# Stacking high and low halves of the step arguments, with a new channel order and re-ordered instruction lists

## The chip, the cores and the metric

The kernel runs on one core of a Trainium2 chip. The metric is the device time of one launch in microseconds (us); it is some 1.8 us longer than the span from the first to the last instruction in the trace. Every kernel was run several times. Each run has a state: "slow" where it lies over 1.5% above the fastest run of the same kernel, "fast" otherwise, and the trace of each run gives the mean clock that TensorE was granted. Comparisons here use fast runs only, unless said. Engines are named as the profile names them: PE is the matmul engine, PEld its weight loads, DVE the vector engine, ACT the scalar engine, POOL GpSimd, SP the queue that issues most DMAs.

## The reference, cut to what matters

The kernel computes a state-space layer as a long convolution, a one-row expert, and a gate:

```python
xn = _layernorm(A_u)                                  # 2048 rows x 512 channels
dt = exp(log_dt)[:, None];  A = A_re + 1j * A_im      # 512 channels x 128 states
P = exp((dt * A)[:, :, None] * arange(2048))          # step arguments dt*A, times the tap number
K = einsum("dn,dnl,dn->dl", Cc, P, dt * Bc).real      # taps
y = irfft(rfft(xn padded to 4096) * rfft(K padded)) + xn * Dskip
g = silu(xn + scatter_add(expert of the one row with the largest xn @ w_r))
return A_u + y * g
```

(The text above shortens the reference; inputs are bf16.) The taps `K` are not computed one by one. An exponent and a sine of `dt*A*l` are factored into products of small tables, and the two Fourier transforms are matmuls against tables.

## The kernel before: the parts that matter here

The kernel is written as a list of operations, and each engine's instruction order is fixed by a hand-tuned list of numbers. A helper at one line (L187) issues almost every matmul, so the profile shows them by their tiles. Four parts matter.

The step arguments are `dt*A`, which bf16 alone would not hold precisely enough. So a high half and a low half (the rest) are made for each group of channels, and a matmul adds them up in PSUM, once per half:

```python
for gp in range(4):
    ts(AD[:, pi, 0, gp, :], S[:, gp, :], DT4[:, gp:gp + 1], MUL, 128, 4)                        # high
for gp in range(4):
    stt(AD[:, pi, 1, gp, :], S[:, gp, :], DT4[:, gp:gp + 1], AD[:, pi, 0, gp, :], MUL, SUB, 128) # low
# ...
def args(pi, c, pair):
    q, js = c // 2, c % 2
    rs = slice(32 * q, 32 * q + 32)
    for gp in range(4):
        o = sap(PB, 0, 128, 512 * (2 * pair + gp // 2) + 16 * (gp % 2), [[32, 16], [1, 16]])
        for hl in range(2):
            mms.append((o, AD[rs, pi, hl, gp, :], IDIJ[rs, 16 * js:16 * js + 16, :], hl == 0, hl == 1))
```

`PB` is the kernel's one PSUM tile, declared as 128 partitions by eight banks of 512 fp32 words; `sap(tile, partition, partitions, offset, pattern)` writes an access pattern by hand as steps and counts.

The taps come out of `kgen` into `KT`, are turned once more through PSUM, and are copied to `KT2` in SBUF as bf16:

```python
for nj, bank in ((6, 4), (5, 5), (5, 4)):
    # ... matmuls of GG and QQ into PB[:, bank]
    act(KT[:, :, j0:j0 + nj], PB[:, bank, 0:80 * nj].rearrange("p (a b) -> p b a", b=80), ACT.Copy, 80 * nj)
# ...
act(KT2[:, q, :, 64 * js:64 * js + 64], PB[:, 5, 0:320].rearrange("p (t c) -> p t c", t=5), ACT.Copy, 320)
```

The profile leaves buffer numbers out, so `KT2` is printed as `KT`.

The spectrum of the taps is 640 matmuls of `KT2` by the table `W` (rows `PB<-KT,W`), each with 128 output columns; ACT then copies a bank pair to `K2T`, DVE multiplies it by the signal's spectrum (`PAB<-U,K2T`), and further matmuls (`PB<-PAB,FA`) transform back:

```python
kp, ip = 1, 3
def pos(pair, i):
    return PB[:, 2 * pair + nd * i // 512, nd * i % 512:nd * i % 512 + nd]
for u2 in range(nu):
    for ro in range(2):
        for k in range(5):
            mms.append((pos(kp, 2 * u2 + ro), W[:, nu * tg + u2, ro, k, :],
                        sap(KT2, 0, 128, d0 // 128 * 640 + 128 * k, [[640, nd // 128], [1, 128]]), k == 0, k == 4))
act(ko, PAIR[kp].rearrange("p a b -> p (a b)"), ACT.Copy, 1024)
```

Here the output, `pos(...)`, is a run of 128 neighbouring fp32 words.

The last part is the tail: after the last inverse transform, a result `ZT` goes to DRAM (`scr_z`), is read back transposed (`DD`), goes through the last matmuls and the gate, and is written out.

Of the kernel before, what the change touches and what calls it, by code (L numbers as in the profile page):

```python
# [8 lines left out]
ALU = mybir.AluOpType  # L9
# [40 lines left out]
class _Graph:  # L50
# [154 lines left out]
    def dma(self, eng, pairs, **kw):  # L205
        fns, outs, ins = [], [], []
        nd = 0
        cost = 0.0
        for dst, src, *ft in pairs:
            fns.append(lambda e, dst=dst, src=src: e.dma_start(dst, src))  # L210
            outs.append(ft[0] if ft else dst)
            ins.append(ft[1] if ft else src)
            cnt = 1
            for s, c in list(dst.ap):
                cnt *= c
            run = min(_run(dst), _run(src))
            nd += cnt // run
            cost += cnt // run * max(33.0, 8.0 + run * mybir.dt.size(dst.dtype) / 25.0) / 16.0
        each = 500.0 if eng == PO else 450.0
        n = self.add(eng, fns, outs, ins, each * len(pairs) + (0.3 * nd if eng == PO else 0.0), dma=True, nbytes=cost, **kw)  # L220
        n.nd = nd
        return n

    def schedule(self):
# [12 lines left out]
        for _ in nodes:  # L237
# [6 lines left out]
            if n.dma:  # L244
                a = max(dma_free[e], n.end)
                dma_free[e] = a + n.nbytes + sum(min(n.nbytes, max(0.0, dma_free[o] - a)) for o in ENGS if o != e)
                n.end = dma_free[e] + 2000.0
# [146 lines left out]

def _pstart(ap):
    return ap.offset // _row(ap.tensor)

_FILL = [(6, 2, 5), (7, 2, 2), (34, 4, 2), (44, 4, 3), (45, 4, 3), (52, 4, 5), (55, 4, 1), (69, 2, 2), (70, 2, 1),
         (107, 4, 1), (129, 4, 2), (216, 2, 6)]
_ORDER = {  # L400
    "sync": [
        11, 0, 1, 2, 12, 10, 15, 3, 13, 14, 5, 4, 8, 9, 16, 6, 7, 152, 157, 162, 167, 324, 325, 326, 308, 327, 323, 318, 313,
        353, 373, 363, 383, 516, 547, 513, 515, 548, 452, 462, 514, 482, 472, 559, 666, 667, 566, 635, 645, 655, 665, 678, 754,
        786, 785, 764, 774, 784, 805, 807, 806, 808, 685, 804, 797, 821, 830,],
    "scalar": [
        20, 21, 44, 52, 53, 56, 23, 55, 48, 58, 59, 62, 61, 50, 108, 80, 109, 81, 119, 130, 121, 129, 149, 172, 169, 127, 151,
        154, 175, 159, 178, 181, 156, 184, 187, 164, 190, 305, 161, 273, 166, 274, 310, 307, 312, 315, 290, 289, 317, 241, 320,
        329, 279, 322, 333, 331, 232, 337, 230, 237, 243, 341, 281, 283, 412, 413, 286, 287, 295, 297, 299, 335, 302, 339, 303,
        348, 428, 343, 358, 352, 429, 368, 418, 420, 422, 362, 425, 426, 434, 436, 438, 441, 442, 378, 372, 486, 494, 495, 447,
        533, 535, 536, 457, 382, 539, 538, 467, 541, 542, 451, 492, 545, 544, 546, 550, 549, 461, 551, 477, 594, 593, 518, 471,  # L410
        610, 609, 481, 522, 599, 520, 601, 603, 712, 606, 607, 615, 526, 617, 713, 619, 524, 530, 622, 623, 528, 668, 630, 669,
        670, 640, 728, 532, 810, 650, 634, 729, 644, 718, 660, 720, 722, 654, 726, 725, 734, 736, 738, 741, 749, 664, 759, 788,
        753, 769, 763, 779, 742, 773, 783, 787, 789, 809, 811, 818, 814, 823, 827,],
    "vector": [
        65, 22, 25, 24, 27, 28, 26, 31, 30, 29, 66, 69, 63, 70, 67, 93, 64, 68, 91, 95, 97, 94, 92, 98, 96, 33, 99, 71, 34, 72,
        100, 42, 73, 101, 35, 74, 102, 37, 104, 76, 32, 105, 77, 41, 38, 106, 78, 36, 107, 79, 39, 46, 43, 40, 82, 103, 75, 45,
        110, 87, 83, 84, 86, 90, 89, 113, 85, 123, 122, 88, 111, 124, 125, 134, 133, 115, 131, 136, 112, 135, 132, 138, 114,
        140, 142, 137, 118, 139, 247, 141, 116, 144, 146, 143, 147, 145, 249, 248, 117, 250, 252, 251, 253, 254, 255, 256, 192,
        193, 257, 258, 194, 259, 196, 198, 199, 200, 201, 260, 203, 261, 205, 206, 262, 276, 264, 263, 265, 266, 211, 267, 268,
        210, 275, 270, 292, 269, 271, 207, 208, 277, 291, 228, 229, 233, 231, 234, 238, 240, 284, 293, 300, 414, 415, 416, 386,  # L420
        388, 387, 389, 390, 391, 392, 394, 393, 395, 396, 397, 349, 398, 350, 399, 400, 401, 402, 403, 359, 404, 360, 405, 406,
        407, 409, 408, 410, 385, 430, 423, 431, 432, 369, 370, 439, 484, 379, 380, 487, 488, 498, 490, 489, 499, 496, 501, 497,
        500, 507, 502, 503, 504, 505, 449, 506, 567, 511, 448, 508, 509, 512, 510, 569, 568, 570, 572, 571, 458, 573, 574, 575,
        459, 576, 577, 578, 469, 579, 580, 581, 582, 468, 583, 584, 595, 585, 554, 587, 586, 479, 557, 588, 478, 590, 596, 589,
        561, 591, 597, 564, 612, 604, 611, 613, 714, 562, 620, 555, 558, 686, 688, 687, 689, 691, 690, 692, 693, 694, 565, 695,
        715, 696, 697, 625, 698, 716, 631, 699, 673, 700, 701, 632, 676, 703, 702, 704, 706, 705, 680, 641, 642, 707, 709, 708,
        710, 683, 652, 651, 731, 723, 730, 732, 662, 661, 739, 751, 750, 677, 681, 674, 761, 760, 770, 771, 780, 781, 744, 802,
        799, 800, 792, 795, 684, 796, 803, 793, 819, 820, 815, 816, 824, 828, 829, 825,],
    "gpsimd": [
        17, 221, 213, 222, 223, 212, 19, 215, 214, 220, 235, 18, 244, 245, 246, 552, 671, 812, 790,],  # L430
    "tensor": [
        51, 54, 47, 57, 60, 49, 128, 120, 148, 150, 171, 168, 126, 153, 170, 174, 177, 158, 173, 180, 176, 155, 183, 179, 186,
        182, 163, 185, 189, 188, 304, 160, 191, 272, 165, 195, 309, 197, 306, 288, 202, 314, 204, 311, 209, 316, 319, 216, 217,
        218, 219, 224, 225, 226, 227, 278, 328, 321, 411, 332, 330, 336, 334, 282, 340, 236, 239, 242, 280, 285, 294, 296, 298,
        427, 301, 338, 346, 344, 345, 347, 342, 354, 356, 355, 357, 351, 364, 366, 367, 365, 384, 361, 374, 417, 419, 376, 421,
        375, 424, 433, 377, 435, 437, 371, 440, 493, 483, 485, 443, 445, 446, 444, 381, 534, 455, 453, 454, 456, 537, 491, 463,
        465, 466, 464, 540, 450, 473, 543, 475, 553, 460, 474, 476, 592, 556, 517, 470, 608, 560, 480, 521, 563, 598, 519, 600,
        602, 711, 525, 605, 614, 616, 618, 529, 523, 727, 621, 527, 628, 629, 626, 627, 624, 672, 636, 638, 639, 637, 531, 675,
        646, 648, 649, 647, 679, 633, 656, 657, 682, 643, 658, 717, 659, 719, 721, 653, 724, 733, 735, 737, 663, 740, 745, 747,
        748, 746, 757, 755, 758, 756, 752, 767, 765, 766, 768, 762, 775, 776, 777, 778, 772, 782, 743, 801, 791, 794, 798, 817,  # L440
        813, 822, 826,],
# [113 lines left out]
def build(nc, A_u, A_A_re, A_A_im, A_B_re, A_B_im, A_C_re, A_C_im, A_log_dt, A_Dskip,  # L555
# [27 lines left out]
    with g.ctx:  # L583
# [35 lines left out]
        LD4 = place("LD4", [128, 4], BF16)  # L619
        DT4 = place("DT4", [128, 4], F32)  # L620
# [24 lines left out]
        ERU = place("ERU", [128, 4, 1408], BF16, o_w + 29696)  # L645
        WD = place("WD", [128, 11, 512], BF16, o_w + 29696)
        ERG = place("ERG", [128, 4, 1408], BF16, o_w + 40960)
# [4 lines left out]
        SAI = place("SAI", [128, 4, 128], BF16, o_b + 8192)  # L652
        EP1 = place("EP1", [128, 4, 256], F32, o_b + 9216)
        WW1 = place("WW1", [128, 2, 256], F32, o_b + 13312)
        UPD = place("UPD", [16, 512], BF16, o_b + 13312)
        SN1 = place("SN1", [128, 4, 256], F32, o_b)
        CN1 = place("CN1", [128, 4, 256], F32, o_b + 4096)
        CS1 = place("CS1", [128, 2, 256], F32, o_b + 7168)
        ZA1 = place("ZA1", [128, 256], F32, o_b + 8192)
        ZB1 = place("ZB1", [128, 256], F32, o_b + 15360)  # L660
# [3 lines left out]
        T1 = place("T1", [128, 2, 256], F32, o_k)  # L664
        T2 = place("T2", [128, 2, 256], F32, o_k + 2048)
# [3 lines left out]
        AD = place("AD", [128, 2, 2, 4, 128], BF16)  # L669
        o_q = cur[0]  # L670
        QQ = place("QQ", [128, 2, 2, 64, 32], BF16)
        WW0 = place("WW0", [128, 2, 256], F32, o_q + 8192)
        ZB0 = place("ZB0", [128, 256], F32, o_q + 8192 + 2048)
        o_g = cur[0]
        EP0 = place("EP0", [128, 4, 256], F32, o_g)
        SN0 = place("SN0", [128, 4, 256], F32, o_g + 4096)
        CS0 = place("CS0", [128, 2, 256], F32, o_g + 8192)
        CN0 = place("CN0", [128, 4, 256], F32, o_t)
        ZA0 = place("ZA0", [128, 256], F32, o_t + 4096)
        POW = ((EP0, SN0, CN0, WW0, (ZA0, ZB0), CS0), (EP1, SN1, CN1, WW1, (ZA1, ZB1), CS1))  # L680
        GG = place("GG", [128, 1, 2, 20, 128], BF16)
        KP = place("KP", [128, 2, 64], BF16)
# [44 lines left out]
        def ts(o, a, s1, op, n, mode=1, s2=None, op2=None):  # L727
            ins = [a] + ([s1] if not isinstance(s1, (int, float)) else [])
            if len(ins) > 1 and mode == 4:
                n, mode = 40 + 1.55 * n, 4  # L730
# [589 lines left out]
```

## Time and profile before

| | before |
|---|---|
| time, median of 4 runs | 198.47 us (197.09 to 200.85) |
| span in the trace | 198.6 us, granted clock 0.925 (a further run, of 200.38 us) |
| first spectrum group starts | 78.80 us |
| last inverse burst starts | 181.14 us |
| PE busy between these | 91.67 of 102.30 us |

The traced run, at 200.38 us, lies 1.7% above the fastest of the four. It is 2.4 us longer than the mean of the three fast ones (198.01), and so may its stretches be in all. The rows of the groups of instructions that the change touches most are these. The columns are line, engine, operation, output and inputs, shapes, count; then busy us and mean ns of one; then the idle time just before these instructions and what ended it.

```profile
L187 PE MATMUL PB<-KT,W 128*128 128x128 bf16 x640 | 39.7, 219 | 2.7 <-ACT K2T L754 1.7 <-ACT KT L754 0.5 <-ACT KV L754 0.2
L187 PE MATMUL PB<-CA,AD 32*128 32x256 bf16 x128 | 20.9, 317 | 8.2 <-DVE AD L738 6.5 <-ACT EE L754 0.8 <-ACT QQ L754 0.8
L725 DVE TENSOR_TENSOR PAB<-U,K2T 128x1024 bf16<-128x1024 bf16 x32 | 21.2, 685 | 12.8 <-ACT K2T L754 11.8 <-DMA scr_a<-AT 1.0
```

The spectrum and the argument matmuls are the two large consumers of PE. The mean of 219 ns is not the distance between two matmuls, as they overlap: a burst of 40 at 78.80 us lasts 2.41 us, and with some 0.22 us for the last one that is 56 ns from one to the next. DVE waits 12.8 us before these products, 11.8 of it for a spectrum that is not there yet, so DVE isn't what holds this stage.

### The profile page before, as it was taken

The page shows a single profiled execution, that of the slowest core. Times are in us where ns is not written, and L with a number is a line of the kernel's source. Part 1 is how long each engine was busy: PE and PEld are TensorE (multiplying, and loading weights), DVE is VectorE, ACT ScalarE, POOL GpSimd, SP SyncE. Part 2 cuts the span into 40 slices and gives each one's busy share as a digit, 9 for nine tenths or more (in the row PEclk, how much of TensorE's full clock was granted, in tenths as well). Part 3 has the DMA queues.
Part 4 walks back from the last instruction along what each step waited for, and adds up shares of the span by engine and source line. Part 5 has one row for each costly group of instructions (what it writes and reads, how often), then busy time and mean ns, then how long its engine had stood idle before and what let it go on. Part 6 is the DMA issues. An engine that isn't in the chain of part 4 may idle for free.

```text
span 198.6 us, 5566 instructions
## 1 busy us (share of the span) xinstructions
PE 165.8 (83%) x2411; PEld 120.2 (61%) x2411; DVE 143.5 (72%) x339; ACT 144.7 (73%) x186; POOL 13.9 (7%) x24
## 2 busy tenths in 40 slices
PE   0697997799998779888999985998899987896960
PEld 0463665555865247877887853676677866894320
DVE  2889889986940239799389999778999980633473
ACT  2298599996749197775799999889969793656440
POOL 0046000000050200000000000200020030000000
PEclk9999999996969957999999999579999999998597
DMA  5979943336969999410031696542833249467965
GB/s 147 333 228 413 418 187 106 108 95 168 316 201 332 430 394 395 133 42 16 3 76 36 163 333 174 153 125 63 263 78 90 56 103 209 119 168 209 226 158 144
DMA packets 40666, 36.79 MB, mean 185 GB/s; under 512 B 26593, under 2 KB 35938, under 8 KB 39746
## 3 DMA queue, kind: packets, MB, share of 16 engines
q1 hardware_dynamic: 38178, 22.25, 39.0%
q0 software_dynamic: 2464, 14.19, 19.9%
q8 instruction: 19, 0.31, 0.6%
q14 instruction: 5, 0.04, 0.1%
HBM read 25.95 MB, written 10.49 MB: 183 GB/s over the span
## 4 chain that ended last, share of the span: by engine, by line
PE 36%; DVE 21%; ACT 18%; DMA 17%; issue 2%; SPq 2%; DVEq 0%; ACTq 0%
PE PB L187 33%; DMA scr_a<-AT 10%; ACT AT L754 4%; ACT XT L957 4%; DVE TT L725 4%; DVE PAB L725 4%; ACT KT L754 4%; DMA X<-in_A_u_dram 3%; DVE ST L802 3%; DVE GG L725 2%; SPq L210 2%; DMA DD<-scr_z 2%; PE PB L280 2%; ACT K2T L754 2%; ACT QQ L754 2%
## 5 line engine op out<-in xcount | busy, mean ns | idle before, releaser
L187 PE MATMUL PB<-KT,W 128*128 128x128 bf16 x640 | 39.7, 219 | 2.7 <-ACT K2T L754 1.7
L187 PEld LDWEIGHTS PB<-KT,W 128*128 128x128 bf16 x640 | 35.9, 98 | 6.1 <-ACT K2T L754 3.4
L187 PE MATMUL PB<-CA,AD 32*128 32x256 bf16 (+1 forms) x192 | 25.9, 357 | 9.9 <-DVE AD L738 8.2
L725 DVE TENSOR_TENSOR PAB<-U,K2T 128x1024 bf16<-128x1024 bf16 x32 | 21.2, 685 | 12.8 <-ACT K2T L754 11.8
L725 DVE TENSOR_TENSOR TT<-GG,ZB 128x512 bf16<-128x512 bf16 (+2 forms) x64 | 27.8, 470 | 0.6
L187 PEld LDWEIGHTS PB<-CA,AD 32*128 32x128 bf16 x192 | 17.4, 129 | 16.7 <-DVE AD L738 9.1
L754 ACT ACTIVATE K2T<-PB 128x1024 bf16<-128x1024 f32 x16 | 16.4, 1022 | 10.6 <-PE PB L187 10.6
L754 ACT ACTIVATE KT<-PB 128x400 bf16<-128x400 f32 (+2 forms) x32 | 18.4, 576 | 5.9 <-PE PB L187 5.2
L187 PE MATMUL PB<-PAB,FA 64*128 64x128 bf16 x512 | 18.7, 228 | 2.1 <-DVE PAB L725 2.1
L725 DVE TENSOR_TENSOR QQ<-QQ,EE 128x2048 bf16<-128x2048 bf16 x16 | 19.5, 1219 | 0.2
L754 ACT ACTIVATE ZT<-PB 128x1024 bf16<-128x1024 f32 x16 | 16.3, 1018 | 4.2 <-PE PB L187 4.1
L187 PEld LDWEIGHTS PB<-PAB,FA 64*128 64x128 bf16 x512 | 15.8, 100 | 5.3 <-DVE PAB L725 2.4
L754 ACT ACTIVATE AT<-PB 128x1024 bf16<-128x1024 f32 x16 | 16.5, 1074 | 1.9 <-PE PB L187 1.8
L754 ACT ACTIVATE U<-PB 128x1024 bf16<-128x1024 f32 x16 | 16.1, 1027 | 1.8 <-PE PB L187 1.6
L725 DVE TENSOR_TENSOR GG<-TT 128x512 bf16<-128x512 bf16 (+2 forms) x32 | 15.1, 472 | 0.6
L754 ACT ACTIVATE EE<-PB 128x1024 bf16<-128x1024 f32 x16 | 15.4, 1035 | 0.0
L187 PE MATMUL PB<-GG,QQ 128*128 128x80 bf16 x256 | 14.2, 213 | 1.4 <-ACT XSEL L754 0.7
L187 PE MATMUL PB<-DD,CB 128*128 128x512 bf16 x32 | 10.9, 458 | 4.4 <-DVE TF L725 2.3
L187 PEld LDWEIGHTS PB<-GG,QQ 128*128 128x128 bf16 x256 | 11.9, 106 | 4.0 <-ACT XSEL L754 1.0
L187 PE MATMUL PB<-XN,CB 128*128 128x256 bf16 (+1 forms) x80 | 12.8, 297 | 1.3 <-ACT AT L754 1.3
L802 DVE BATCH_NORM_STATS2 ST<-X 128x6 f32<-128x512 bf16 x16 | 9.9, 683 | 5.1 <-DMA X<-in_A_u_dram 5.1
L280 PE MATMUL PB<-CA 128*128 128x512 bf16 x33 | 13.3, 524 | 0.1
(131 smaller groups left out, 225.1 us busy)
## 6 DMA issues: line engine op xcount, KB each, us to landing
W<-c_w POOLq DMA_DIRECT2D x4, 1280.0 KB, 10.0
scr_a<-AT SPq DMA_DIRECT2D x8, 512.0 KB, 6.0
BT<-scr_a SPq DMA_DIRECT2D x8, 512.0 KB, 5.3
scr_z<-ZT SPq DMA_DIRECT2D x16, 256.0 KB, 3.5
DD<-scr_z SPq DMA_DIRECT2D x6, 512.0 KB, 5.1
XR<-in_A_u_dram POOLq DMA_DIRECT2D x4, 512.0 KB, 6.0
out_dram<-XR SPq DMA_DIRECT2D x8, 256.0 KB, 2.9
X<-in_A_u_dram SPq DMA_DIRECT2D x3, 512.0 KB, 6.6
```

Of the source, the lines that this page charges most:

```text
L187: fns.append(lambda e, o=o, l=l, r=r, st=st, sp=sp, tp=tp: e.matmul(o, lhsT=l, rhs=r, start=st, stop=sp, tile_position=tp, skip_group_chec ...
L210: fns.append(lambda e, dst=dst, src=src: e.dma_start(dst, src))
L280: n.fns = [lambda e, o=o: e.matmul(o, lhsT=lhs, rhs=rhs, start=True, stop=True, tile_position=(0, 0), skip_group_check=True)] * k
L725: g.V(lambda e: e.tensor_tensor(out=o, in0=a, in1=b, op=op), [o], [a, b], n, mode)
L754: nd = g.A(lambda e: e.activation(out=o, in_=i, func=func, **kw), [o], ins, n + (110 if "bias" in kw else 0), after=[ph["pre"]] if tab els ...
L802: g.V(lambda e, b=b: e.bn_stats(ST[:, b, :], X0[:, b, :]), [ST[:, b, :]], [X0[:, b, :]], 512)
L957: g.A(lambda e, pv=pv, xt=xt: e.activation(out=xt, in_=pv, func=ACT.Copy), [XT[:, bq % 2]], [PB[:, bank, :]], 1024)
```

## The change

The intent is to shorten PE's work on the arguments. The high and low halves of `dt*A` are placed on different partitions of one tile, so that one matmul over 64 rows adds both, and two groups of channels run in two row tiles at a time. The taps are copied in two pieces instead of three per chunk, an extra product on DVE goes, layernorm and power operations are merged, and the power stages, the sines and the expert move ahead of the first spectrum. The stacked load brings the channels in as even ones, then odd ones, and this order is undone where the spectrum is written. The core of the diff, with cuts marked:

```diff
+        def sload(S, A):
+            for gh, eng in ((0, SP), (1, AC)):
+                g.dma(eng, [(S[64 * gh + 32 * hl:64 * gh + 32 * hl + 32].rearrange("p (q e) n -> p q (e n)", q=4),
+                             dap(A, 8192 * gh, [[256, 32], [16384, 4], [1, 256]])) for hl in range(2)])
 ...
+            for c in range(8):
+                act(HH[:, pi, c, :], S[:, c, :], ACT.Copy, 128, scale=DTS[:, c:c + 1])
+                stt(AD[:, pi, c, :], S[:, c, :], DTM[:, c:c + 1], HH[:, pi, c, :], MUL, SUB, 128)
 ...
         def args(pi, c, pair):
-            (four groups, high and low half: eight matmuls of 256 columns)
+            g.M([(PB[:, 2 * pair + gh, :], AD[64 * gh:64 * gh + 64, pi, c, :], IDIJ[64 * gh:64 * gh + 64, :, :], True, True) for gh in range(2)])
 ...
         def kgen(c):
-            for nj, bank in ((6, 4), (5, 5), (5, 4)):
+            for hg in range(2):
 ...
-            tt(kp, gl, sap(QQ, 0, 128, 4096 * qb + 31, [[2048, 2], [32, 64]]), MUL, 128, 1)
 ...
         def spec(pt):
-                kp, ip = 1, 3
+                kp, ip = (2 if pt == 3 and tg % 2 else 1), 3
 ...
-                            mms.append((pos(kp, 2 * u2 + ro), W[:, nu * tg + u2, ro, k, :],
+                            mms.append((sap(PB, 0, 128, 1024 * kp + nd * (2 * u2 + ro), [[1, 2], [2, 64]]), W[:, nu * tg + u2, ro, k, :],
 ...
 (program: bcw(1), powers(1), the sines and the expert before the first f2 and spec; all five lists of instruction order replaced)
```

(The line in parentheses under `args` stands for six removed lines, and so does the last one for the order of calls and the lists.)

## The prediction

> **What bounds the kernel now.** I read the engines' shares first, then busy time by stretch, then the chain of waits, then single bursts in the timeline. The page's first part:
>
> ```profile
> PE 165.8 (83%) x2411; PEld 120.2 (61%) x2411; DVE 143.5 (72%) x339; ACT 144.7 (73%) x186; POOL 13.9 (7%) x24
> ```
>
> No engine is full over the whole span, so I cut it where the character changes: the first spectrum burst (PB<-KT,W, the taps times the table W) starts at 78.80 us, the last inverse burst (PB<-PAB,FA) at 181.14. Columns: stretch, length, then busy us and instruction count for each engine, granted clock, DMA share, GB/s.
>
> ```profile
> core 0: us, PE busy (x) PEld busy (x) DVE busy (x) ACT busy (x) POOL busy (x), PEclk, DMA share, GB/s
> 3.60:78.80 75.20, 63.74 (x685) 41.81 (x686) 54.68 (x161) 55.58 (x72) 9.06 (x16) 0.91 0.77 274
> 78.80:181.10 102.30, 91.67 (x1662) 74.30 (x1660) 81.16 (x161) 82.13 (x104) 4.63 (x4) 0.97 0.46 125
> 181.10:198.60 17.50, 10.34 (x66) 4.11 (x66) 7.67 (x18) 5.70 (x9) 0.00 (x0) 0.74 0.70 173
> ```
>
> The reader should see that in the middle stretch, over half of the kernel, PE is busy 91.67 of 102.30 us, at nearly full clock: it is the fullest engine there, and DVE and ACT have 21 and 20 us to spare. The first stretch is a mix (loads, layernorm, the router and the expert, waits for DMA); the last is a serial tail. The chain that ended last shows how the middle hands over to the tail (start, length, what):
>
> ```profile
> 172.77 2.42 PE PB L187 x40
> 175.21 1.03 ACT K2T L754
> 176.29 2.42 PE PB L187 x40
> 178.74 1.03 ACT K2T L754
> 179.79 1.30 DVE PAB L725 x2
> 181.14 1.09 PE PB L187 x32
> 182.25 1.03 ACT ZT L754
> 183.30 2.98 DMA scr_z<-ZT
> 186.30 4.39 DMA DD<-scr_z
> ```
>
> A spectrum group is 40 matmuls, then ACT's copy of its bank pair; the next group waits for that copy, since there is one pair. After the last group some 20 us follow whatever else happens.
>
> The lines that decide my prediction are bursts of matmuls in the timeline (start, length of the burst, shapes, count):
>
> ```profile
> 78.80 2.41 PE L187 MATMUL PB<-KT,W 128*128 128x128 bf16 x40
> 89.00 1.07 PE L187 MATMUL PB<-PAB,FA 64*128 64x128 bf16 x32
> 94.65 0.60 PE L187 MATMUL PB<-GG,QQ 128*128 128x80 bf16 x12
> 98.28 1.05 PE L187 MATMUL PB<-CA,AD 32*128 32x128 bf16 x16
> 100.02 0.62 PE L187 MATMUL PB<-DG,STG 64*128 64x64 bf16 x8
> 100.45 0.63 PE L187 MATMUL PB<-CA,STG 64*128 64x64 bf16 x8
> 111.89 1.04 PE L187 MATMUL PB<-CA,AD 32*128 32x256 bf16 x8
> ```
>
> A burst's length is its steps plus the last matmul's own latency (about 0.2 us). Spectrum: (2.41 - 0.22) / 39 = 56 ns for 128 columns. GG,QQ: (0.60 - 0.21) / 11 = 35 ns for 80. Arguments with 256 columns: about 107 ns. These write contiguous runs of PSUM and all come to 0.42 ns per column. The DG,STG and CA,STG bursts write every fourth fp32 word: 100.02 to 100.45 is 8 steps, 54 ns for only 64 columns. The 98.28 burst, also every fourth word, is eight pairs in two row tiles: (1.05 - 0.31) / 7 = 106 ns per pair, so 106 ns for 128 columns in each tile. That is 0.83 ns per column: strided PSUM output runs at half rate.
>
> [...] no burst before has a step of two. [...] different row tiles overlap; the FA burst shows it: (1.07 - 0.2) / 31 = 28 ns for 128 columns in two alternating tiles, half of 56.
>
> **The change part by part.**
>
> *Step arguments.* High and low halves of dt*A now lie in 64 stacked rows, so one matmul sums them. An argument block was 8 matmuls of 256 columns (0.97 us to the next burst, 111.89 to 112.86) and becomes 2 of 512 in two row tiles, about 0.22 us by 0.42 ns per column: -0.75 x 16 = -12 us of PE work, half of it in the middle stretch. The power arguments go from 16 strided to 8 contiguous matmuls: about 0.9 to 0.23 us, x4 = -2.7. ACT gets 16 small HH copies (about 0.3 us) and loses one 0.64 us copy: +4 us, all at the start. DVE gets 16 instead of 8 fused operations (349 ns each, +2.8) and loses 8 tensor_scalar operations (-2).
>
> *Half-width tap copies.* KT is read in 2 copies of 640 columns per chunk, not 3 (480 + 400 + 400): -8 copies' fixed cost, from 14.9 us (8 x 0.57 + 16 x 0.645) to about 16 x 0.72 = 11.5, -3.4 on ACT. KP's product goes: -3.0 on DVE.
>
> *Merged layernorm and power operations.* About 12 tiny operations (0.15) and some fixed costs: -3 on DVE. DVE in all about -5 of 143.5, ACT about even.
>
> *What the new channel order adds.* The stacked load leaves the taps as even channels, then odd. The interleave is undone in the output of the spectrum matmuls: their PSUM access pattern becomes (2, 64) with a step of two words. There are 640 of them. At 0.83 ns per column each takes 109 instead of 56 ns: +53 x 640 = +34 us of PE work, nearly all in the stretch where PE already leads. This is the largest single number in the change.
>
> *Order.* Powers for both halves, chain and sines of pair 1 and the expert come before the first spectrum group. The middle stretch loses DVE work: one GG chain ((27.8 + 15.1) / 4 = 10.7), three QQ products (3.7) and the second power stage (about 9), but the first stretch gains it, so its DVE goes from 55 to some 70 us. With the start and the waits for X, the first group then comes at 77 to 84, about where it was. In the last part (pt 3) a second bank pair takes the ACT copy off the chain: about -1 us x 3, now outweighed by groups of 4.4 us.
>
> **Sum.** Middle PE: 91.7 + 34.2 - 5.9 (8 argument blocks) - 2.6 (second powers) - 2.5 (fills, moved output transforms) = 115 busy. Some of 91.7 is latency that a fuller queue covers, and some waits (9.2 us idle now) stay: 112 to 120 long instead of 102. Start about 79, plus 114, plus the tail of 17: 210 us.
>
> **The rivals.** (1) A step of two words is not slowed, as it is not the measured step of four. Then PE's middle falls to about 80, DVE's to 60 and ACT's to 75; at the present fullness the stretch is near 88 us, and 79 + 88 + 17 = 184. For it: all lists were re-ordered, which a kernel's author would do only with a gain in view; the new lists price no stride. Against it: three kinds of strided burst give the same half rate[...]. (2) The half rate is real but hides behind ACT and DVE, as PE only waits for them: about 197 us. Against it: PE has 10 us idle in the middle, and 34 - 11 must go somewhere. (3) The lists were timed for 56 ns groups, so every consumer of a spectrum now comes late and PE, in strict order, then blocks argument and tap work behind it: 216 or more. (4) Earlier weight loads relieve the 20.5 us DMA wait (scr_a, from 62.8 us); this takes up to 5 us off the start: 205.
>
> **Range and chances.** Half rate at a step of two: about 0.83, allowing for the fact that someone chose this version. Given it, 210 with some 6 us either way, slower by over 2% (201.4) in nearly nine of ten. Without it, near 184. So 0.17 faster, 0.11 within 2%, 0.72 slower; the range 194 to 219 leaves out the fast case.
>
> **What would show it.** Right: the KT,W row's mean goes from 219 to about 310 ns and its busy time from 39.7 to about 70 us, a burst of 40 lasts 4.5 us, PE's share rises above 88%, the CA,AD rows shrink to under 10 us, and DVE is at most 70% busy. Wrong: KT,W still steps by 56 ns; or the first spectrum group starts well before 72 us; or PE is idle over 20 us in the middle although the groups are slow.

## The result

| | before | after |
|---|---|---|
| median | 198.47 us | 217.06 us |
| runs | 197.48, 197.09, 200.85, 199.47 | 213.9, 220.07, 214.05, 220.62 |

The two runs of after near 214 are fast (clock 0.960 and 0.965), the two near 220 slow (0.914 and 0.940). The ratio of after to before is 1.0806, with a 95% interval of 1.0641 to 1.0971: slower. A ratio is the mean time of one kernel's fast runs over the mean of the other's fast runs in the same rounds, so it is not quite the ratio of the medians quoted beside it.

The profile after is of a fast run, with a span of 212.1 us. First the shares of the engines:

```profile
PE 170.0 (80%) x2286; PEld 132.5 (62%) x2286; DVE 142.3 (67%) x321; ACT 144.9 (68%) x192; POOL 14.1 (7%) x24
```

PE does 4.2 us more than before with 125 instructions fewer. Its share fell, from 83 to 80%, which looks like an engine that got less important. The stretches show that this is wrong. They are cut as before (start of the first spectrum group, start of the last inverse burst); columns are the stretch, its length, busy us and instruction count of PE, PEld, DVE, ACT and POOL, granted clock, DMA share, GB/s.

```profile
3.60:82.03 78.43, 51.54 (x653) 31.91 (x653) 68.51 (x181) 64.88 (x93) 9.29 (x16) 0.93 0.78 256
82.03:194.16 112.13, 109.70 (x1571) 97.30 (x1570) 62.95 (x118) 73.25 (x91) 4.63 (x4) 1.00 0.43 120
194.16:212.10 17.94, 8.76 (x66) 3.33 (x66) 10.72 (x24) 5.50 (x8) 0.00 (x0) 0.81 0.79 177
```

In the middle PE is now busy 109.70 of 112.13 us, 98%. DVE and ACT have 49 and 39 us to spare there. Of the 13.5 us by which the span grew, 3.2 came in the start (78.43 against 75.20), 9.8 in the middle (112.13 against 102.30) and 0.4 in the tail. Between the means of the fast runs the growth is 16.0 us (213.98 against 198.01), as the traced run of before is among its longer ones; which stretch holds the other 2.5 us the traces don't tell.

The groups that answer to those of before:

```profile
L187 PE MATMUL PB<-KT,W 128*128 128x128 bf16 x640 | 74.5, 313 | 0.3 <-ACT K2T L758 0.2
L187 PE MATMUL PB<-CA,AD 64*128 64x512 bf16 x32 | 7.3, 455 | 17.0 <-DVE AD L742 15.5 <-ACT EE L758 0.9 <-ACT QQ L758 0.6
L729 DVE TENSOR_TENSOR PAB<-U,K2T 128x1024 bf16<-128x1024 bf16 x32 | 21.5, 688 | 30.1 <-ACT K2T L758 30.1
L758 ACT ACTIVATE K2T<-PB 128x1024 bf16<-128x1024 f32 x16 | 16.4, 1024 | 24.2 <-PE PB L187 24.2
```

The same 640 spectrum matmuls, with the same shapes and the same count, are busy 74.5 instead of 39.7 us. The arguments shrank as intended. The idle columns show who leads: DVE waits 30.1 us for ACT's spectrum copy, ACT waits 24.2 us for PE, and PE waits almost for nothing (0.3).

The bursts in the timeline (start, length, shapes, count) show the distance from matmul to matmul:

```profile
83.55 2.36 PE L187 MATMUL PB<-KT,W 128*128 128x128 bf16 x20
86.32 1.25 PE L187 MATMUL PB<-KT,W 128*128 128x128 bf16 x10
```

Ten more matmuls add 2.36 - 1.25 = 1.11 us: 111 ns each, where it was 56. The clock doesn't explain it: in this stretch the granted clock is 1.00, against 0.97 before. The chain of waits that ended last, near its end (start, length, what), no longer alternates between PE and ACT. It is long runs of PE:

```profile
108.88 24.14 PE PB L187 x311
...
141.21 50.52 PE PB L187 x648
191.75 1.03 ACT K2T L758
...
196.32 2.88 DMA scr_z<-ZT
199.21 4.89 DMA DD<-scr_z
```

Its start shows a wait that the chain of before does not have:

```profile
3.54 8.46 DMA AR<-in_A_A_re_dram
12.02 3.03 ACT HH L758 x10
```

The stacked load of A lands at 12.0 us, and ten HH copies follow before the first exponential. The first argument matmul starts at 13.65 us; before, it started at 6.46. The first spectrum group, 68 us later, is only 3.2 us late, so this wait need not be what costs the time.

### The profile page after: what moved, and what is told of

It reads as the page before. It is cut to its first block, busy times and chain, and to the rows that moved or that the text cites.

```text
span 212.1 us, 5296 instructions
## 1 busy us (share of the span) xinstructions
PE 170.0 (80%) x2286; PEld 132.5 (62%) x2286; DVE 142.3 (67%) x321; ACT 144.9 (68%) x192; POOL 14.1 (7%) x24
## 4 chain that ended last, share of the span: by engine, by line
PE 60%; ACT 21%; DMA 8%; DVE 7%; issue 1%; SPq 1%; DVEq 0%
PE PB L187 58%; DMA AR<-in_A_A_re_dram 4%; ACT AT L758 4%; ACT XT L967 3%; ACT EE L758 3%; DMA DD<-scr_z 2%; DVE TT L729 2%; ACT U L758 2%; ACT HH L758 2%; PE PB L281 2%; ACT K2T L758 2%; ACT SC L758 1%; ACT ZT L758 1%; DMA scr_z<-ZT 1%; ACT KT L758 1%
## 5 line engine op out<-in xcount | busy, mean ns | idle before, releaser
L187 PE MATMUL PB<-KT,W 128*128 128x128 bf16 x640 | 74.5, 313 | 0.3 <-ACT K2T L758 0.2
L187 PEld LDWEIGHTS PB<-KT,W 128*128 128x128 bf16 x640 | 67.2, 135 | 3.3 <-issue 0.9
L729 DVE TENSOR_TENSOR PAB<-U,K2T 128x1024 bf16<-128x1024 bf16 x32 | 21.5, 688 | 30.1 <-ACT K2T L758 30.1
L758 ACT ACTIVATE K2T<-PB 128x1024 bf16<-128x1024 f32 x16 | 16.4, 1024 | 24.2 <-PE PB L187 24.2
L187 PE MATMUL PB<-CA,AD 64*128 64x512 bf16 (+1 forms) x64 | 9.2, 358 | 17.8 <-DVE AD L742 16.3
L758 ACT ACTIVATE KT<-PB 128x640 bf16<-128x640 f32 (+1 forms) x24 | 14.9, 619 | 7.6 <-PE PB L187 7.4
L187 PE MATMUL PB<-PAB,FA 64*128 64x128 bf16 x512 | 17.1, 217 | 0.9 <-DVE PAB L729 0.9
L187 PEld LDWEIGHTS PB<-CA,AD 64*128 64x128 bf16 x64 | 2.7, 104 | 22.3 <-DVE AD L742 17.3
L187 PEld LDWEIGHTS PB<-PAB,FA 64*128 64x128 bf16 x512 | 14.4, 94 | 3.5 <-issue 1.5
L729 DVE TENSOR_TENSOR TF<-PB,XN 128x512 bf16<-128x512 f32 x12 | 8.1, 686 | 9.1 <-PE PB L187 7.3
L187 PE MATMUL PB<-DD,CB 128*128 128x512 bf16 x32 | 9.3, 407 | 4.3 <-DMA DD<-scr_z 2.7
L187 PE MATMUL PB<-GG,QQ 128*128 128x80 bf16 x256 | 12.2, 200 | 0.5 <-ACT KT L758 0.5
```

The lines of the kernel that those rows point to most:

```text
L187: fns.append(lambda e, o=o, l=l, r=r, st=st, sp=sp, tp=tp: e.matmul(o, lhsT=l, rhs=r, start=st, stop=sp, tile_position=tp, skip_group_chec ...
L729: g.V(lambda e: e.tensor_tensor(out=o, in0=a, in1=b, op=op), [o], [a, b], n, mode)
L758: nd = g.A(lambda e: e.activation(out=o, in_=i, func=func, **kw), [o], ins, n + (110 if "bias" in kw or isinstance(kw.get("scale"), bass.A ...
```

## The experiments

Twelve runs follow, of ten kernels (contig ran three times). All results were correct except for two that give a wrong result (said there). The theory was that the one line which writes the spectrum with a step of two words costs more than everything else in the change gains. The rivals were that the new order of the lists, or the later start, or the removed slack, is what costs.

### contig: the spectrum written contiguously

The de-interleave moves from PE's output to ACT's copy of the taps, which writes even and odd channels with a step of two bf16 elements:

```diff
-act(KT2[:, q, :, 64 * js:64 * js + 64], PB[:, 5, 0:320]...)
+act(KT2[:, q, :, js:128:2], PB[:, 5, 0:320]...)
-mms.append((sap(PB, 0, 128, 1024 * kp + nd * (2 * u2 + ro), [[1, 2], [2, 64]]), W[...]
+mms.append((pos(kp, 2 * u2 + ro), W[...]
```

> The changed kernel with one thing undone: the spectrum matmuls write contiguous PSUM runs again, and the interleave of even and odd channels is made by ACT, which writes the taps KT2 with a step of two bf16. Right result expected. Theory A (half-rate PSUM writes fill PE's middle stretch): the KT,W row goes back from 313 to about 219 ns, a step from 109 to 56 ns, the middle stretch from 111 us to about 90, the time to about 192 (188 to 197), so faster than the kernel before by 1 to 5%. Rival B (the new lists and the late start cause the loss, the strided output only a part): over 205. The KT2 copies on ACT should keep their 445 ns; if a strided bf16 write costs ACT, they grow.

Measured: 189.94 us median (186.12 to 192.33), ratio to before 0.9368 (0.9279 to 0.9456): faster than both kernels. Its two fast runs are 186.12 and 187.64 us. The same kernel was run twice more for comparison, as contig2 and contig3.

> The contiguous version again, beside the next one on the same chip: 0.93 to 0.95 of the kernel before, about 187 in fast runs.

> The contiguous-output form of the changed kernel once more, only to stand on the same chip as the next two: both theories expect 184 to 190 us (medians before 189.94 and 186.93), faster than the kernel before by 5 to 7%.

Measured: 186.93 us (ratio 0.9412, 0.9327 to 0.9498; mean of the fast runs 185.26) and 190.02 us (ratio 0.9531, 0.9446 to 0.9615; mean of the fast runs 189.20). All three intervals end below 0.97. The three calls were on different chips, so a ratio of this kernel carries a scatter of 1.7% between calls, and its profiles fell in the slow state each time (clock 0.88 to 0.91). The rows of contig2, from a run of 187.85 us:

```profile
L187 PE MATMUL PB<-KT,W 128*128 128x128 bf16 x640 | 41.5, 223 | 0.2 <-ACT K2T L758 0.2
82.68:162.93 80.25, 77.34 (x1571) 66.11 (x1570) 62.11 (x117) 72.11 (x91) 4.64 (x4) 0.98 0.53 149
162.93:186.00 23.07, 11.59 (x66) 3.75 (x66) 10.91 (x24) 5.61 (x8) 0.00 (x0) 0.68 0.88 201
```

The middle is 80.25 us long, 32 us shorter than after's and 22 us shorter than before's, and PE is still the fullest engine (77.34 us). The slow state does not explain this: in pairs_only below, whose traced run is fast, the same stretch is 80.1 us (80.82 to 160.91). So the rest of the change shortens the middle. What is given back shows in the other two stretches: the first spectrum comes at 82.68 us instead of before's 78.80, and the tail takes 23.1 instead of 17.5 us (22.6 in pairs_only).

### before_strided_only: the step alone, on the kernel before

The reverse test: the old kernel, its order and lists untouched, with only the output pattern of the spectrum changed. Its result is wrong (channels land in the wrong places).

```diff
-mms.append((pos(kp, 2 * u2 + ro), W[...]
+mms.append((sap(PB, 0, 128, 1024 * kp + nd * (2 * u2 + ro), [[1, 2], [2, 64]]), W[...]
```

> The kernel before with nothing changed but the PSUM pattern of its 640 spectrum matmuls (step of two words). Wrong result on purpose: the channels come out permuted, as the KT2 write is left alone, whose permuted form cost ACT 1.17 us more in each of 8 copies in the earlier run (1616 against 445 ns). Theory A: PE alone explains the loss, 34 us less what its 9 us of idle time absorbs: 224 to 233 us. Rival D (the ACT copies made a good part of the earlier 240): under 218.

Measured: 228.62 us (226.81 to 230.03), ratio 1.164 (1.1535 to 1.1745).

```profile
L187 PE MATMUL PB<-KT,W 128*128 128x128 bf16 x640 | 73.8, 313 | 2.8 <-ACT K2T L754 1.7 <-ACT KT L754 0.5 <-ACT KV L754 0.2
81.25 4.54 PE L187 MATMUL PB<-KT,W 128*128 128x128 bf16 x40 [0.56 <-ACT K2T L754]
```

A burst of 40 lasts 4.54 instead of 2.41 us. The row gained 34.1 us of busy time, and the time 31.8 us (fast runs: mean 228.52, all four, against 196.75). In the changed kernel the same line costs 28.7 us (fast runs of after, mean 213.98, against those of contig2, mean 185.26; other chips). So the step is the cause, with or without the new lists.

### before_strided: the same with a correct result

Here ACT's copy into `KT2` puts the channels into even-odd order, so that the strided output is right again.

```diff
-act(KT2[:, q, :, 64 * js:64 * js + 64], PB[:, 5, 0:320]...)
+act(sap(KT2, 0, 128, 640 * q + 32 * js, [[128, 5], [1, 32], [64, 2]]), PB[:, 5, 0:320]...)
```

> The kernel before, with the changed kernel's output pattern (2 x 64, step of two words) in its 640 spectrum matmuls, and ACT's KT2 write permuted so that the result stays right; lists, arguments and all else as before. Theory A: 53 ns more for each of 640 matmuls, 34 us of PE work in a stretch with 9 us of idle PE: 220 to 232 us, some 11 to 17% slower. Rival B (lists made for another order take the damage): under 208.

Measured: 239.74 us (237.44 to 242.01; the two fast runs 237.53 and 237.44), above the expected range and more than the step explains. The spectrum row is busy 76.9 us, but the eight permuted copies also grew, from 0.444 to 1.616 us each, because neighbouring elements now land 64 bf16 elements (128 bytes) apart. That is 9.4 us of ACT right before the spectra. It was a flaw of the experiment, and before_strided_only was made to take it out.

### pairs: runs of two words

If what counts is a pair of neighbouring words and not a fully contiguous output, then a pattern that writes two words, skips two and comes back should run at full rate.

```diff
-[[1, 2], [2, 64]]
+[[2, 2], [4, 32], [1, 2]]
 (and a copy into KT2 that puts the channels in matching order, with an inner step of 64 elements)
```

> The changed kernel with a spectrum output that is still permuted, but in runs of two fp32 words (pattern 2 x 32 x 2 with steps 2, 4 and 1), and ACT's KT2 write permuted to match; right result expected. Theory A1 [...]: full rate, 56 ns steps, and the time of the contiguous version within 1%. Rival A2 (any pattern that is not one run is slow): 109 ns steps and the changed kernel's time, about 214.

Measured: 196.63 us (193.12 to 197.98). Its one fast run, 193.12, is 3% above contig's fast runs on the same chip (mean 186.88), so the time missed the expected 1%. The matmuls are at full rate again (42.2 us busy, 225 ns in the mean), and the copy has the same flaw as above:

```profile
L758 ACT ACTIVATE KT<-PB 128x320 bf16<-128x320 f32 x8 | 13.0, 1624 | 0.9 <-PE PB L187 0.7
```

### pairs_only: the same without the slow copy

The copy into `KT2` is left as in the changed kernel, so the result is wrong.

> The changed kernel with the spectrum output in runs of two words and the KT2 write as in the changed kernel, plain. Wrong result on purpose (permuted channels). Theory A1: the PSUM pattern of two-word runs costs nothing, so with the slow KT2 copies (1624 ns) gone the time is the contiguous version's, 186 to 190, also 1 us under it since the KT2 write has no step of two. Rival: if two-word runs still cost something that the matmul rows hide, it stays at 193 or over.

Measured: 186.61 us over all four runs, the fast two 185.25 and 184.32; contig2's fast runs on the same chip have a mean of 185.26.

```profile
81.81 1.29 PE L187 MATMUL PB<-KT,W 128*128 128x128 bf16 x20
L758 ACT ACTIVATE KT<-PB 128x320 bf16<-128x320 f32 x8 | 3.6, 445 | 0.5 <-PE PB L187 0.3
```

The row `PB<-KT,W` is at 40.3 us and 219 ns; a burst of 20 lasts 1.29 us against 2.36. A step inside a pattern is thus not slow as such: runs of two words are as fast as 128 in a row (a burst of 20 takes 1.29 us in contig2 too, at 88.69 us), single words two apart run at half rate. All pairs here start at an even word; whether a pair that starts at an odd word would do as well was not tried.

### half: only the first two of four parts strided

```diff
-mms.append((pos(kp, 2 * u2 + ro), W[...]
+mms.append((sap(PB, ..., [[1, 2], [2, 64]]) if pt < 2 else pos(kp, 2 * u2 + ro), W[...]
 (the copy into KT2 has the step of two only for parts 2 and 3, which are as in contig)
```

> The changed kernel with the strided output in parts 0 and 1 only (320 of the 640 matmuls), contiguous in parts 2 and 3. Theory A with PE full all through the middle: the cost is linear, so halfway between the contiguous version and the changed kernel, about 203. Rival C (one stretch alone is bound by PE): near one of the two ends, under 197 or over 210.

Measured: 205.5 us (204.67 to 205.82, all fast), ratio 1.0306 (1.024 to 1.0372).

```profile
84.20:180.42 96.22, 93.73 (x1570) 81.89 (x1570) 62.41 (x116) 72.56 (x91) 4.64 (x4) 0.99 0.43 122
```

From the first spectrum group to the last inverse burst it takes 80.3 us with none strided (contig2), 96.2 with half, and 112.1 with all (after). That is 16.0 and 15.9 us for 320 matmuls each, or 50 ns for one. The cost is in proportion, so the step costs work, not a new wait. The times don't divide as evenly (186.9 for the fast runs of contig on the same chip, 205.4 for half, 214.0 for after). In the traces the rest of the unevenness lies outside the middle: the first group starts at 82.7, 84.2 and 82.0 us, and the tails are 23.1, 22.5 and 17.9 us.

### The later start: contig_params_first, contig_dts_first, contig_params_dts_first

Three runs tried to win back the start, all based on contig. The first puts the loads of `A` and `dt` ahead of those of the input X in the SP and ACT lists; no code changes.

```diff
-        14, 0, 15, 17, 1, 4, 7, 3, 19,     (SP)       5, 24, 2, 26, 41,   (ACT)
+        0, 1, 14, 3, 4, 15, 17, 7, 19,     (SP)       2, 5, 24, 26, 41,   (ACT)
```

> The contiguous version with the stacked step parameters issued ahead of the inputs X (lists of SP and ACT only): in the changed kernel their second half was issued at 3.06 us behind two loads of X and landed at 12.0, where ACT waited for it 6.8 us. Theory: ACT's first HH copy moves from about 11 or 12 to about 6, and with it the first spectrum group by 2 to 4 us: 184 us, 1 to 2% under the contiguous version. Rival: the layernorm, which now gets X later, and the router behind it set the start, so within 1%, or slower.

Measured: 190.92 us (189.71 to 191.4, all fast), ratio 0.9704 (0.9646 to 0.9762), slower than contig2 (fast runs 190.77 against 185.26). The expectation missed. The trace says why (timeline of ACT at the start; the wait in brackets):

```profile
11.86 1.86 ACT L758 ACTIVATE HH<-AR,DTS 128x128 bf16<-128x128 bf16 x6 [7.63 <-DVE DTS L736]
```

`A` was there, but the small DVE copies that make `DTS` stand behind layernorm statistics in DVE's fixed list, and these wait for X, which now comes later. So the next two put the DTS and DTM copies first in DVE's list, once with contig's load order and once with the one just tried.

```diff
-        25, 91, 30, 31, 92, 93, 28, 27, 32, 94, 101, 99, 29, 49,     (DVE)
+        25, 27, 28, 30, 31, 29, 32, 91, 92, 93, 94, 101, 99, 49,
```

> Contiguous output, and on the vector engine's list the six small copies that widen dt (DTS, DTM) stand ahead of the layernorm statistics, which wait for X; load orders as in the changed kernel. Theory A (in this load order ACT's first HH copies wait for the load of AR, not for DTS): no gain, within 1% of the plain contiguous form. Theory B (DVE's strict order is what holds the start in either load order): the first matmul 2 us or more earlier and 2 to 4 us off the time.

> The same list for the vector engine with the load orders of the run that was slower than expected (AR, AI and dt ahead of X). Theory A (that run lost because the DTS copies stood behind layernorm statistics waiting for X): HH's wait for DTS, 7.6 us there, falls under 2 us, HH starts 2 to 4 us earlier, and the time falls at least 2 us below that run's 190.9, to 183 to 188. Rival (the later X holds layernorm and router, and these set the start of the spectra): the wait is gone, but the time stays at 189 to 192.

Measured: contig_dts_first 186.85 us, ratio 0.9377 (0.9295 to 0.9459); contig_params_dts_first 188.49 us, ratio 0.9386 (0.9275 to 0.9497); contig3 0.9531 (0.9446 to 0.9615). With contig's load order the first matmul starts at 12.30 instead of 12.72 us, so the 2 us of theory B are not there. Yet on the same chip the fast runs are 3.1 us shorter (mean 186.15 against 189.20, and the ranges don't overlap), more than the 1% of theory A. Both theories missed in part, and what gained the time stays open: the two traces, both of slow runs, have the first spectrum group at 83.99 and 85.67 us, and the starts of one kernel scatter by more than that. With parameters first, the wait for DTS is gone, and another has taken its place:

```profile
5.17 1.86 ACT L758 ACTIVATE HH<-AR,DTS 128x128 bf16<-128x128 bf16 x6 [0.95 <-DMA AR<-in_A_A_re_dram]
13.95 0.98 ACT L758 ACTIVATE HH<-AI,DTS 128x128 bf16<-128x128 bf16 x3 [6.92 <-DVE AI L736]
```

The first six copies start at 5.17 us instead of 11.86. The next wait for DVE to strip the sign of A's imaginary part, an operation that also stands behind the layernorm statistics. The first matmul comes at 14.23 us, 0.6 us earlier than in contig_params_first (14.87). The wait moved instead of falling. The median, 188.49, is just above the expected range because three of the six runs are slow; the three fast ones (mean 186.34) lie in it, level with contig_dts_first, so the load order brought nothing more.

### contig_out_late: what makes the tail longer

The last write of z took 7.32 us in contig2 and 9.18 in contig, against 2.88 in after. This kernel issues the two output writes of the first part after the last reads of z.

```diff
-        701, 708, 769, 770, 738, 748, 758, 768, 789, 790, 791, 792, 721,     (SP)
+        769, 770, 738, 748, 758, 768, 789, 790, 791, 792, 701, 708, 721,
```

> Contiguous output, and the two output writes of the first part (they stand on the sync queue right before the last part's z writes and reads) are issued after the last reads of z. Theory (the tail of the contiguous form is longer than that of the changed kernel because output writes still occupy the DMA engines when the last z write starts): the last z write falls from 7.3 to 9.2 us to 3 to 5 us, and 1 to 4 us come off, a ratio to the kernel before of about 0.92 to 0.935. Rival (what slows it are the four z writes themselves, the reads of z and the loads of the inputs, all close together because the groups now come faster): the last z write stays above 6 us, and the time is within 1% of the contiguous form (ratio 0.937 to 0.953) or worse, as two writes more stand at the end.

Measured: 200.95 us (195.34 to 202.02). Only one of six runs is fast; at 195.34 it is 1.2% under the fast runs of the kernel before (mean 197.74), far from contig's 5 to 6%. The chain at its end:

```profile
166.21 2.77 DMA scr_z<-ZT
...
169.83 5.99 DMA out_dram<-XR
176.10 6.20 DMA XR<-in_A_u_dram
```

The first half of the theory held: the last z write takes 2.77 us. But a later part's input is loaded into the buffer that the moved write empties. That load now starts at 176.10 us, and the chain goes write, load, gate; the tail is 33 us. As both the writes and the load left the window of the z write, this run doesn't tell which of them had slowed it. It does show that the outputs can't simply be put off.

One more variant, contig with a single bank pair throughout, could not be built: with these fixed lists its instructions wait for each other in a circle. It wasn't run, so the worth of the second pair stays open.

## Why the prediction was right, and where it was off

The predicted 210 us is 7 below the median of 217.06, which mixes two fast and two slow runs, and 4 below the fast ones; both are inside the range; "slower" was given 0.72. The mechanism it named, half rate at a step of two words, is what the runs show, by adding it alone (1.164) and by taking it out of the changed kernel (0.937 to 0.953). That the sum came so close is partly luck: it was built from stretches of the trace, and there 79 + 114 + 17 stands against 82.0 + 112.1 + 17.9 = 212.1, a start 3 us too short beside a middle 2 us too long.

**Spectrum matmuls: right.** Predicted were 109 ns, a mean of about 310, about 70 us busy and +34 us. Measured were 111 ns, 313, 74.5 and +34.8. The transfer of a step of four words, seen in small bursts, to a step of two was the author's estimate, as no burst of before has a step of two; it held. (By the bursts that the prediction shows, contiguous output takes 0.42 to 0.44 ns per column: 107 ns for 256, 35 for 80, 56 for 128. Its 109 ns is an estimate too, between 128 x 0.83 = 106 and twice 56.)

**Arguments and powers: right.** The step predicted -12 and -2.7 us, and the `CA,AD` rows to fall below 10 us. With both shapes in one row they fell from 25.9 to 9.2 us, 16.7 instead of 14.7 (by shape 20.9 and 7.2 before, 7.3 and 2.0 after, which counts overlaps twice). The 16 tap copies of 640 columns, put at 0.72 us each, took 0.706; by before's copies (444 ns for 320 columns, 1022 for 1024) one would take 0.707.

**Middle stretch: right in kind, one term too small.** Predicted were 115 us busy in 112 to 120; measured 109.70 in 112.13. The spectrum term is right to 0.6 us, so the miss is in what goes: 34.8 came and 18.0 is the rise, so 16.8 went, where 11.0 was predicted. For arguments and powers in this stretch the prediction took off 5.9 + 2.6 = 8.5; the argument row fell by 7.1 (10.2 to 3.1) and the power matmuls with `STG` by 1.2 (0.6 twice, moved to the start), 8.3 together. For "fills, moved output transforms" it took 2.5. That is the mis-sized term: some 8.5 us went. The largest parts are the output matmuls `DD,CB` (5.2 to 2.7), the inverse matmuls `PAB,FA` (17.6 to 16.0, with the same 480, in the mean 217 instead of 229 ns) and the table matmuls of `CA` (1.0, moved to the start). The tap product `KP,CB` (1.3) went, but `KT,CA` grew by about as much (2.9 to 4.4).

**Start: the term of the sum that was too small.** "The first group then comes at 77 to 84" held, at 82.0, but the sum took 79. The prediction counted DVE's extra work and the waits for X. It did not see that the stacked load lands only at 12.0 us and that ACT's HH copies wait 6.8 us for it. Its price for these copies was right: ten in a row take 3.03 us, about 0.30 each. The rows show a mean of 387 and 392 ns for one, more than the 303 ns from one to the next, so they overlap. For comparison, the copies of 128 columns in before (`XN<-XSEL`, L1186) took 307 ns in the mean.

Whether the wait for `AR` costs the 3 us is not shown. With that load moved ahead (contig_params_dts_first) HH starts at 5.17 us, DVE's list holds the next copies, and the first spectrum group still comes at 85.96. The size itself is uncertain: up to the first group, before_strided_only is the same code as before, and its first group comes at 75.60 instead of 78.80. In the kernels with after's lists (after, the three contig runs, half, pairs_only) it comes at 80.82 to 85.67. So the start did get longer, by an amount that one trace of each kernel does not fix.

**Tail: nearly right.** 17 predicted, 17.9 measured.

**"PE's share rises above 88%": wrong.** It is 80%, because PE is less busy in the start (51.54 of 78.43 us, before 63.74 of 75.20). A share of the whole span averages over stages. In the stage concerned it is 98%.

**The rivals.** Rival 1, no slowing at a step of two, had the right picture of a kernel without the slow pattern: 184 predicted for it, and contig's fast runs are 184.36 to 190.06. Its middle was put at 88 and is 80.3 in contig2, which the longer start and tail offset. Rival 2, the half rate hides behind ACT and DVE, fell: DVE and ACT have 49 and 39 us to spare in the middle. Rival 3, PE blocks work behind late spectra, isn't supported: PE idles 2.4 us there. Rival 4, earlier weight loads shorten the start, isn't seen: the start got longer.

**Where the gain went.** The change without the strided output gains 5 to 6%: by the traces 22 us in the middle against before, less 4 us of start and 5.6 us of tail. The step of two then costs 32 us of the middle. The best correct kernel is contig (perhaps a little better with the DVE list of contig_dts_first): it keeps every idea of the change and de-interleaves in ACT's eight copies, which costs 95 ns each (540 against 445), where PE paid 55 ns on each of 640 matmuls.

## What to carry to other kernels

When data comes in a shuffled order, ask which operation undoes it the fewest times: eight copies with a small step cost under 1 us in all, 640 matmul outputs with a step cost 34. Price an access pattern like an instruction: the cost function of the list scheduler here counts a matmul's columns and not the step of its output, so it could not see this. And read the busiest engine by stage, since its share of the whole span can fall while it becomes the full bound of the stage that matters.

## Figures that these runs give

- Matmuls with 128 output columns, from one to the next: 111 ns with single words at a step of two (after), 56 ns with 128 words in a row (before). Runs of two words with gaps between them run at full rate (a burst of 20 in 1.29 us in pairs_only, as in contig2, which writes contiguously).
- An ACT copy of 320 columns from PSUM to bf16 took 445 ns contiguous (after, pairs_only), 540 with a step of two elements (contig2), and 1616 to 1624 where neighbours land 128 bytes apart (before_strided, pairs).
- The last write of z, 256 KB to DRAM, took 2.77 to 2.98 us in before, before_strided_only, after and contig_out_late, 6.09 in half, 6.56 in pairs_only, 7.32 in contig2 and 9.18 in contig. What makes it longer, no run here shows.
